# A decode attention kernel: the score products of a tile of keys in two halves, each on two column groups

## The chip, the cores and the metric

The kernel runs on one core of one Trainium2 chip. The core's engines work side by side, each through its own list of instructions in order, and wait for one another by semaphores. TensorE (PE) multiplies matrices into PSUM and loads its stationary operand with instructions of its own (PEld). VectorE (DVE) transposes and reduces, ScalarE (ACT) takes the exponential, SyncE (SP) issues the transfers from the chip's memory. The metric is the device time of one launch in microseconds (us), the median of the runs that are shown. An execution that the hardware profiler recorded gives the profile; its span runs from the first to the last instruction.

## The reference

One decode step for two batch rows: attention over the last 4,096 keys of a cache (32 query heads, 8 heads of keys and values) beside a gated feed-forward layer, both on the same normalised input, summed onto the input.

```python
xn = _layernorm(x)
q = (xn @ wq).reshape(B, Sq, Hq, Dh).transpose(0, 2, 1, 3)      # B=2, Sq=1, Hq=32, Dh=128
k = repeat(k_cache[:, :, Sk - W:, :], 4, axis=1)                # W=4096, 8 heads of keys
v = repeat(v_cache[:, :, Sk - W:, :], 4, axis=1)
p = softmax(einsum("bhqd,bhkd->bhqk", q, k) * Dh ** -0.5)
o = einsum("bhqk,bhkd->bhqd", p, v)
gate = xn @ W_gate; up = xn @ W_up
return x + o.reshape(B, Sq, Hq * Dh) @ wo + ((gate * (gate > 0)) * up) @ W_down
```

Everything is in 4-byte floats.

## The kernel before

All large inputs come through a ring of four buffers (`RING = 4`), each for one load of up to 4 MB, in the order in which they are used: wq in two loads, W_gate, W_up, then for each of four groups g two key tiles k and two value tiles v, then W_down and wo in two (the second in four pieces). SP issues a load when the buffer four loads earlier has been read for the last time: a key tile's buffer is free after its transposes, a value tile's after its products.

A group is one batch row with four of the eight heads of keys. Its score work runs over two key tiles, a = 0 and 1 (`scores`, L291). A key tile has 128 partitions of 64 positions by 128 numbers. DVE transposes it in 32 by 32 blocks, in two halves s1 = 0 and 1 (`S1` is 2) of two instructions each (L301), into a tile kT; kT has two buffers (`ktp`), so the halves of the next key tile write over those of this one, and must wait until PE has read them.

The products of q with a half are eight matmuls of 128 rows by 32 columns by 512 (L311): four blocks cb of the head dimension, which are summed, times two halves h of the positions. Each matmul appears twice in the trace, as PE takes two passes for it. The result lands in 32 of the 128 partitions of the scores tile ss[g], from `lo = 32 * (2 * s1 + h)` on. These four places are four column groups of the PE array: those of half 0 are groups 0 and 1, those of half 1 are groups 2 and 3. Matmuls on different column groups can run at the same time.

The order is that of the code (`manual_schedule`). Before, all four transposes of a key tile are issued, and then the sixteen matmuls with cb outermost, s1 next and h innermost, so that four in a row lie on the four column groups.

After the second key tile of a group follow the maximum over the scores (L319), a small chain through PE, DVE and ACT to the exponential (L340), a reordering product with a transpose (L346, L348), and for each value tile the products with p (`values`, L361). `gather` (L370, L376) masks and folds the result of a value tile, `finish` (L385, L386) scales it. The last gather and finish of a group are put into the list `late`, and run inside the next group's first call of `scores`, between the transposes of its first and second half. After group 1 the list also holds `spread_heads` (L391, L396), a set of small matmuls on PE and a copy on DVE.

At the end come the products with W_down and wo into y4 (L429), the last ones into y_ps (L436), a copy and the store.

Of the kernel before, what the change touches and what calls it, by code (L numbers as in the profile page):

```python
# [20 lines left out]
def kernel(  # L21
# [28 lines left out]
    S1 = W // (Q * 512)  # L50
    L = 32
    PB = P // L
    CB = DH // L
# [77 lines left out]
    qz = const.tile([P, NG, CB, 2, ZW], F32, name="qz")  # L131
# [98 lines left out]
    for r in range(R):  # L230
# [15 lines left out]
        for b in range(B):  # L246
            for pb in range(PB):
                rows = slice(L * pb, L * pb + L)
                for a in range(NP):
                    lo = 2 * a * 16 + pb * REP  # L250
# [35 lines left out]
    ss, pts, rls = {}, {}, {}  # L286
# [4 lines left out]
    def scores(g, a, kt_in):  # L291
        if a == 0:
            ss[g] = ps_s.tile([P, 512], F32, name=f"s{g}", tag="s")
        kts = []
        for s1 in range(S1):
            kt = ktp.tile([P, JH, CB, KL, 2], F32, name=f"kT{g}_{a}_{s1}", tag="kT")
            kts.append(kt)
            for n in range(2):
                lo = JH // 2 * n
                j = JH * s1 + lo  # L300
                nc.vector.transpose(  # L301
                    kt[:, lo:lo + JH // 2].rearrange("p j c k h -> p (j c k h)"),
                    kt_in[:, j * DH:(j + JH // 2) * DH],
                )
            while late:
                late.pop(0)()
        for cb in range(CB):
            for s1 in range(S1):
                for h in range(2):
                    lo = 32 * (2 * s1 + h)  # L310
                    nc.tensor.matmul(  # L311
                        ss[g][lo:lo + 32, :], qz[:, g, cb, h, 16 * a:16 * a + 32], kts[s1][:, :, cb, :, h],
                        start=(a == 0 and cb == 0), stop=(a == NP - 1 and cb == CB - 1),
                    )

# [82 lines left out]
    for g in range(NG):  # L398
        kt_in = [load_kv(k_cache, "k", g, a) for a in range(NP)]
        v_in = [load_kv(v_cache, "v", g, a) for a in range(NP)]  # L400
        for a in range(NP):
            scores(g, a, kt_in[a])
        turn(g, *softmax(g, maxima(g)))
        for a in range(NP):
            values(g, a, v_in[a])
            if a + 1 < NP:
                gather(g, a)
        late.append(lambda g=g: (gather(g, NP - 1), finish(g)))
        if g % B == 1 and g + 1 < NG:
            late.append(lambda g=g: spread_heads(g // B))  # L410
# [78 lines left out]
```

## Time and profile before

| | us |
|---|---|
| median of 3 runs | 252.2 |
| lowest and highest | 248.37 and 253.96 |
| the profiled execution | 251.82 |
| its span | 250.0 |
| PE busy, DVE busy | 153.1, 103.0 |
| loads from memory | 94.90 MB, 380 GB/s over the span |
| granted TensorE clock, mean | 0.816 |

The profile names groups of instructions by their line in the kernel, their engine, and the tiles as out<-in. "Idle before" is the time for which the engine stood still just ahead of an instruction, with what ended it. The granted clock is the share of full speed at which the array ran; in this trace it is either 0.50 or 1.00 at any moment. A matmul's shown duration is longer than the distance to the next one on the same column group, because consecutive ones overlap in the array: distances between starts say how fast they pass.

### The profile page before, as it was taken

The page shows a single profiled execution, that of the slowest core. Times are in us where ns is not written, and L with a number is a line of the kernel's source. Part 1 is how long each engine was busy: PE and PEld are TensorE (multiplying, and loading weights), DVE is VectorE, ACT ScalarE, POOL GpSimd, SP SyncE. Part 2 cuts the span into 40 slices and gives each one's busy share as a digit, 9 for nine tenths or more (in the row PEclk, how much of TensorE's full clock was granted, in tenths as well). Part 3 has the DMA queues.
Part 4 walks back from the last instruction along what each step waited for, and adds up shares of the span by engine and source line. Part 5 has one row for each costly group of instructions (what it writes and reads, how often), then busy time and mean ns, then how long its engine had stood idle before and what let it go on. Part 6 is the DMA issues. An engine that isn't in the chain of part 4 may idle for free.

```text
span 250.0 us, 2211 instructions
## 1 busy us (share of the span) xinstructions
PE 153.1 (61%) x948; PEld 49.2 (20%) x948; DVE 103.0 (41%) x121; ACT 8.3 (3%) x27; POOL 8.1 (3%) x31
## 2 busy tenths in 40 slices
PE   0079749316557585544588658185883817588993
PEld 0062342101001230101122321011220101122343
DVE  1220123295671267395225572912188292221201
ACT  0020213000000100000100000001000000100000
POOL 8400000000000000000000000000000000000000
PEclk9999977755757999795958957868599786959999
DMA  7999999999999999999999999999169999946900
GB/s 289 452 435 393 436 440 422 456 446 425 417 415 419 440 456 435 427 419 419 419 440 430 438 440 425 419 398 425 47 252 453 456 399 450 419 176 241 404 28 1
DMA packets 3784, 95.03 MB, mean 380 GB/s; under 512 B 430, under 2 KB 448, under 8 KB 704
## 3 DMA queue, kind: packets, MB, share of 16 engines
q1 hardware_dynamic: 3756, 94.90, 89.3%
q8 instruction: 7, 0.11, 0.2%
q10 hardware_dynamic: 20, 0.01, 0.0%
q14 instruction: 1, 0.01, 0.0%
HBM read 94.90 MB, written 0.00 MB: 380 GB/s over the span
## 4 chain that ended last, share of the span: by engine, by line
PE 49%; DVE 28%; DMA 10%; issue 7%; POOL 3%; ACT 1%; POOLq 0%; ACTq 0%; DVEq 0%
DVE kT L301 19%; PE s L311 16%; PE o L361 14%; DMA k<-in_A_k_cache_dram 10%; PE pp L346 4%; PE y L429 4%; PE oa L376 3%; PE q_ps L224 3%; DVE on L370 2%; DVE pt L348 2%; PE op L391 2%; PE xt_ps L214 1%; ACT p L340 1%; DVE m L319 1%; PE y_ps L436 1%
## 5 line engine op out<-in xcount | busy, mean ns | idle before, releaser
L311 PE MATMUL s<-kT,qz 128*32 128x512 f32 x256 | 56.8, 865 | 49.6 <-DVE kT L301 49.6
L301 DVE STREAM_TRANSPOSE kT<-k 128x2048 f32<-128x2048 f32 x32 | 71.4, 2281 | 21.1 <-PE s L311 18.8
L361 PE MATMUL o<-v,pt 128*32 128x512 f32 x256 | 38.5, 708 | 4.8 <-DVE rl L352 4.8
L311 PEld LDWEIGHTS s<-kT,qz 128*32 128x32 f32 x256 | 11.0, 144 | 91.6 <-DVE kT L301 63.5
L370 DVE TENSOR_TENSOR on<-o,mask 128x512 f32<-128x512 f32 x8 | 5.5, 692 | 26.5 <-PE o L361 26.5
L361 PEld LDWEIGHTS o<-v,pt 128*32 128x32 f32 x256 | 10.6, 128 | 25.8 <-issue 20.6
L214 PE MATMUL xt_ps<-rep,xn 2*128 2x32 f32 x16 | 3.7, 400 | 13.8 <-DVE xn L208 13.8
L346 PE MATMUL pp<-p,perm 128*128 128x512 f32 x16 | 9.3, 707 | 4.7 <-ACT p L340 4.7
L376 PE MATMUL oa<-on,picks 128*16 128x512 f32 x16 | 8.3, 597 | 6.3 <-DVE on L370 6.3
L319 DVE TENSOR_REDUCE m<-s 128x1 f32<-128x512 f32 x4 | 2.8, 692 | 22.5 <-PE s L311 22.5
L348 DVE STREAM_TRANSPOSE pt<-pp 128x1024 f32<-128x1024 f32 x4 | 5.0, 1250 | 13.2 <-PE pp L346 13.2
L224 PE MATMUL q_ps<-wq,xnT 128*32 128x512 f32 x64 | 9.8, 782 | 0.5 <-DVE xnT L216 0.5
L340 ACT ACTIVATE p<-s,nm 128x512 f32<-128x512 f32 x4 | 2.7, 687 | 170.7 <-DVE nm L334 170.7
L214 PEld LDWEIGHTS xt_ps<-rep,xn 2*128 2x128 f32 x16 | 3.6, 320 | 13.8 <-issue 13.8
L251 DVE COPY qz<-rq 32x32 f32<-32x32 f32 x16 | 3.0, 187 | 7.1 <-ACT qz L251 7.1
L391 PE MATMUL op<-osb,spread 16*128 16x32 f32 x32 | 5.0, 314 | 1.1 <-DVE osb L386 1.1
L429 PE MATMUL y<-wo,oT 128*32 128x512 f32 x48 | 5.4, 594 | 0.0
L391 PEld LDWEIGHTS op<-osb,spread 16*128 16x128 f32 x32 | 4.8, 231 | 2.8 <-DVE osb L386 2.0
L239 DVE COPY qT<-qt 128x32 f32<-128x32 f32 x2 | 0.4, 192 | 11.8 <-PE qt L235 11.8
L261 PE MATMUL g_ps<-wg,xnT 128*32 128x448 f32 x32 | 4.8, 762 | 0.0
L385 DVE TENSOR_REDUCE su<-oa 16x128 f32<-16x512 f32 x4 | 2.7, 680 | 4.5 <-PE oa L376 4.5
L429 PE MATMUL y<-wd,hT 128*32 128x512 f32 x28 | 4.5, 595 | 0.0
(79 smaller groups left out, 62.7 us busy)
## 6 DMA issues: line engine op xcount, KB each, us to landing
k<-in_A_k_cache_dram SPq DMA_DIRECT2D x8, 4096.0 KB, 25.9
v<-in_A_v_cache_dram SPq DMA_DIRECT2D x8, 4096.0 KB
wq<-in_A_wq_dram SPq DMA_DIRECT2D x2, 4096.0 KB, 16.9
wo<-in_A_wo_dram SPq DMA_DIRECT2D x1, 4096.0 KB
wg<-in_B_W_gate_dram SPq DMA_DIRECT2D x1, 3584.0 KB
wu<-in_B_W_up_dram SPq DMA_DIRECT2D x1, 3584.0 KB
wd<-in_B_W_down_dram SPq DMA_DIRECT2D x1, 3584.0 KB, 19.3
wo<-in_A_wo_dram SPq DMA_DIRECT2D x1, 2048.0 KB
```

Of the source, the lines that this page charges most:

```text
L214: nc.tensor.matmul(xt_ps[:, o, kc, :], cols, rep.rearrange("r s b -> r (s b)"), start=True, stop=True)
L224: nc.tensor.matmul(q_ps[r][32 * c:32 * c + 32, :], xnT[:, 0, kc, :], wqt[kc // 2][:, kc % 2, n * 512:(n + 1) * 512], start=(kc == 0), stop ...
L301: nc.vector.transpose(kt[:, lo:lo + JH // 2].rearrange("p j c k h -> p (j c k h)"), kt_in[:, j * DH:(j + JH // 2) * DH],)
L311: nc.tensor.matmul(ss[g][lo:lo + 32, :], qz[:, g, cb, h, 16 * a:16 * a + 32], kts[s1][:, :, cb, :, h], start=(a == 0 and cb == 0), stop=(a ...
L319: nc.vector.tensor_reduce(out=m, in_=ss[g], op=ALU.max, axis=AX.X)
L346: nc.tensor.matmul(pp[:, h], perm[:, h], p, start=True, stop=True)
L348: nc.vector.transpose(pts[g].rearrange("p n j k -> p j n k"), pp.rearrange("p h y -> p y h"))
L361: nc.tensor.matmul(o[32 * q:32 * q + 32, :], pts[g][:, a * S1 + s1, j:j + 4, :].rearrange("p u k -> p (u k)"), v[:, lo:lo + 512], start=(s ...
L370: nc.vector.tensor_tensor(ons[a], os[a].rearrange("p (u d) -> p u d", u=4), mask[:, :, None].to_broadcast([P, 4, P]), op=ALU.mult)
L376: nc.tensor.matmul(oa[g], picks[:, a].rearrange("p h a i -> p (h a i)"), ons[a], start=(a == 0), stop=(a == NP - 1))
L391: nc.tensor.matmul(op, spread[:, e].rearrange("h k e -> h (k e)"), osb[r][:, :, e * NJ:(e + 1) * NJ].rearrange("h b j -> h j b"), start=(e ...
L429: nc.tensor.matmul(y4[32 * t:32 * t + 32, :], lhsT.rearrange("p b s -> p (b s)"), w, start=(i < Q), stop=(i >= EARLY - Q))
```

## The change

The products with a half of a key tile are issued right behind the transposes of that half, instead of behind the transposes of both. Where the order was cb, s1, h it is now s1, cb, h: eight matmuls on column groups 0 and 1, then eight on groups 2 and 3. The number of instructions, their shapes and their data stay; so do the lists of DVE and SP, apart from the line numbers.

```diff
     def scores(g, a, kt_in):
         if a == 0:
             ss[g] = ps_s.tile([P, 512], F32, name=f"s{g}", tag="s")
-        kts = []
         for s1 in range(S1):
             kt = ktp.tile([P, JH, CB, KL, 2], F32, name=f"kT{g}_{a}_{s1}", tag="kT")
-            kts.append(kt)
             for n in range(2):
...
             while late:
                 late.pop(0)()
-        for cb in range(CB):
-            for s1 in range(S1):
+            for cb in range(CB):
                 for h in range(2):
                     lo = 32 * (2 * s1 + h)
                     nc.tensor.matmul(
-                        ss[g][lo:lo + 32, :], qz[:, g, cb, h, 16 * a:16 * a + 32], kts[s1][:, :, cb, :, h],
+                        ss[g][lo:lo + 32, :], qz[:, g, cb, h, 16 * a:16 * a + 32], kt[:, :, cb, :, h],
                         start=(a == 0 and cb == 0), stop=(a == NP - 1 and cb == CB - 1),
                     )
```

On PE, the first key tile of group 0 stands in the program before as follows; kT0_0_0 is the first half of its transposed keys and kT0_0_1 the second, s0 the scores of the group, qz the query, and the waits are in brackets:

```order
L311 MATMUL s0_333<-kT0_0_0_334,qz_94 32x512 [waits DVE_49]
L311 MATMUL s0_333<-kT0_0_0_334,qz_94 32x512
L311 MATMUL s0_333<-kT0_0_1_337,qz_94 32x512 [waits DVE_49]
L311 MATMUL s0_333<-kT0_0_1_337,qz_94 32x512
L311 MATMUL s0_333<-kT0_0_0_334,qz_94 32x512 x2
L311 MATMUL s0_333<-kT0_0_1_337,qz_94 32x512 x2
L311 MATMUL s0_333<-kT0_0_0_334,qz_94 32x512 x2
L311 MATMUL s0_333<-kT0_0_1_337,qz_94 32x512 x2
L311 MATMUL s0_333<-kT0_0_0_334,qz_94 32x512 x2
L311 MATMUL s0_333<-kT0_0_1_337,qz_94 32x512 x2
```

Of the eight products with the first half, two stood ahead of the wait for the second half and six behind it. In the changed program the same place on PE, with the second key tile (kT0_1_0 and kT0_1_1) and the transpose of the maximum behind it, reads:

```order
L308 MATMUL s0_333<-kT0_0_0_334,qz_94 32x512 [waits DVE_49]
L308 MATMUL s0_333<-kT0_0_0_334,qz_94 32x512 x7
L308 MATMUL s0_333<-kT0_0_1_345,qz_94 32x512 [waits DVE_49]
L308 MATMUL s0_333<-kT0_0_1_345,qz_94 32x512 x7
L308 MATMUL s0_333<-kT0_1_0_356,qz_94 32x512 [waits DVE_49]
L308 MATMUL s0_333<-kT0_1_0_356,qz_94 32x512 x7
L308 MATMUL s0_333<-kT0_1_1_367,qz_94 32x512 [waits DVE_49]
L308 MATMUL s0_333<-kT0_1_1_367,qz_94 32x512 x7
L318 MATMUL mt0_380<-ident_89,m0_378 1x128 [waits DVE_49]
```

All eight products of a half now stand behind the wait for that half alone.

The second place is on PE where group 2 begins, behind the last fold of group 1 (oa1) and the matmuls of `spread_heads` (op0). Before:

```order
L376 MATMUL oa1_545<-on1_1_576,picks_125 16x512 [waits DVE_49]
L391 MATMUL op0_582<-osb0_456,spread_111 128x32 [waits DVE_49]
L391 MATMUL op0_582<-osb0_456,spread_111 128x32 x7
L311 MATMUL s2_572<-kT2_0_0_573,qz_94 32x512 x2
L311 MATMUL s2_572<-kT2_0_1_592,qz_94 32x512 [waits DVE_49]
L311 MATMUL s2_572<-kT2_0_1_592,qz_94 32x512
L311 MATMUL s2_572<-kT2_0_0_573,qz_94 32x512 x2
```

and in the changed program:

```order
L373 MATMUL oa1_545<-on1_1_576,picks_125 16x512 [waits DVE_49]
L388 MATMUL op0_582<-osb0_456,spread_111 128x32 [waits DVE_49]
L388 MATMUL op0_582<-osb0_456,spread_111 128x32 x7
L308 MATMUL s2_572<-kT2_0_0_573,qz_94 32x512 x8
L308 MATMUL s2_572<-kT2_0_1_600,qz_94 32x512 [waits DVE_49]
L308 MATMUL s2_572<-kT2_0_1_600,qz_94 32x512 x7
```

The first half's products still follow the small matmuls of `spread_heads`, now all eight of them and with no wait of their own.

## The prediction

> **What bounds the kernel now.** I read the chain of waits first, then the groups of instructions, then the timeline of two groups. From the page: the span, what the chain consists of by engine, and the costliest DVE group.
>
> ```profile
> span 250.0 us, 2211 instructions
> PE 49%; DVE 28%; DMA 10%; issue 7%; POOL 3%; ACT 1%; POOLq 0%; ACTq 0%; DVEq 0%
> L301 DVE STREAM_TRANSPOSE kT<-k 128x2048 f32<-128x2048 f32 x32 | 71.4, 2281 | 21.1 <-PE s L311 18.8
> ```
>
> PE and DVE take turns: together 77% of the chain, transfers 10%. The last row says that DVE stood still 18.8 us ahead of key transposes because PE had not yet read the buffer. The timeline of group 0's first key tile and of all of group 1 shows where (start, length, engine, operation, idle time before and its releaser).
>
> ```profile
> 50.55 8.89 DVE L301 STREAM_TRANSPOSE kT<-k 128x2048 f32<-128x2048 f32 x4 [2.36 <-DMA k<-in_A_k_cache_dram]
> 55.12 1.92 PE L311 MATMUL s<-kT,qz 128*32 128x512 f32 x4 [7.78 <-DVE kT L301]
> 59.50 6.17 PE L311 MATMUL s<-kT,qz 128*32 128x512 f32 x28 [2.47 <-DVE kT L301]
> 64.82 8.89 DVE L301 STREAM_TRANSPOSE kT<-k 128x2048 f32<-128x2048 f32 x4 [5.38 <-PE s L311]
> ...
> 97.99 4.49 DVE L301 STREAM_TRANSPOSE kT<-k 128x2048 f32<-128x2048 f32 x2
> 102.53 5.19 PE L311 MATMUL s<-kT,qz 128*32 128x512 f32 x28 [4.63 <-DVE kT L301]
> 106.88 8.89 DVE L301 STREAM_TRANSPOSE kT<-k 128x2048 f32<-128x2048 f32 x4 [4.40 <-PE s L311]
> 111.44 1.12 PE L311 MATMUL s<-kT,qz 128*32 128x512 f32 x4 [3.72 <-DVE kT L301]
> 115.82 5.37 PE L311 MATMUL s<-kT,qz 128*32 128x512 f32 x28 [3.27 <-DVE kT L301]
> 121.25 0.69 DVE L319 TENSOR_REDUCE m<-s 128x1 f32<-128x512 f32 x1 [5.48 <-PE s L311]
> ```
>
> Strict alternation: transposes, then 28 of the 32 matmuls, meanwhile DVE idle (5.38 us in group 0, 4.40 in group 1, by the total (18.8 - 5.38) / 3 = 4.5 in each later group), then transposes again while PE is idle.
>
> The transfers do not set this pace, but they are close. A window of the steady part (DMA share and GB/s last):
>
> ```profile
> 60.00:175.00 115.00, 72.27 (x367) 19.72 (x359) 56.15 (x49) 2.33 (x6) 0.00 (x0) 0.78 1.00 427
> ```
>
> The load of k2_0, with its time from issue to landing,
>
> ```profile
> L73 SPq DMA_DIRECT2D k<-in_A_k_cache_dram x1: 534/534/534, 102.5 to 102.5; - x1
> DMA to landing us min/median/max: 26.1/26.1/26.1
> ```
>
> and that of k3_1:
>
> ```profile
> L73 SPq DMA_DIRECT2D k<-in_A_k_cache_dram x1: 535/535/535, 163.5 to 163.5; - x1
> DMA to landing us min/median/max: 14.1/14.1/14.1
> ```
>
> The DMA engines are busy all of that window at 427 GB/s, so a 4 MB tile (4.19 MB) takes 9.8 us. k2_0 landed at 102.5 + 26.1 = 128.6, and four loads earlier k1_0 at about 89.4. k3_1 landed at 163.5 + 14.1 = 177.6, and k3_0 9.8 earlier at 167.8. The first transposes of groups 1 and 2 started at:
>
> ```profile
> 90.56 2.30 DVE L301 STREAM_TRANSPOSE kT<-k 128x2048 f32<-128x2048 f32 x1
> ...
> 134.80 4.49 DVE L301 STREAM_TRANSPOSE kT<-k 128x2048 f32<-128x2048 f32 x2
> ```
>
> k1_0 was used about 1 us after landing, k2_0 6.2 us after. The ring then ran full; the loads of v3_0 and of wo's second half were issued at:
>
> ```profile
> 182.03 0.54 SPq L73 DMA_DIRECT2D v<-in_A_v_cache_dram  x1
> ...
> 226.40 1.85 SPq L448 DMA_DIRECT2D wo<-in_A_wo_dram  x4
> ```
>
> v3_0 could go only 4.4 us after the last load had landed. Compute is late, and gets later with each group.
>
> **The change part by part.** *How fast a pair runs.* Only two column groups work in a stretch now. The second round of two pairs:
>
> ```profile
> 55.97 1.06 PE L311 MATMUL s<-kT,qz 128*32 128x512 f32 x2
> 111.90 0.66 PE L311 MATMUL s<-kT,qz 128*32 128x512 f32 x2
> ```
>
> Against the starts at 55.12 and 111.44, a round of two takes 0.85 us at clock 0.50 and 0.46 at 1.00. A round of four takes no more: the 28 matmuls from 59.50 are seven rounds of four in 6.17 us, 0.88 each. So half of PE's width is given up: a half is 8 matmuls, 16 passes, eight rounds of two, 7 x 0.46 + 0.66 = 3.9 us at full clock, and 7 x 0.85 + 1.06 = 7.0 at half. It has 4.49 us of transposes (row 97.99) to hide behind: hidden at full clock, not at half.
>
> *Group 1, the model group.* On PE its first products (s) stand behind the last fold of group 0 (oa):
>
> ```profile
> 96.00 0.60 PE L376 MATMUL oa<-on,picks 128*16 128x512 f32 x1 [0.83 <-DVE on L370]
> 96.02 0.62 PE L311 MATMUL s<-kT,qz 128*32 128x512 f32 x1
> 96.44 0.59 PE L376 MATMUL oa<-on,picks 128*16 128x512 f32 x1
> 96.47 1.42 PE L311 MATMUL s<-kT,qz 128*32 128x512 f32 x3
> ```
>
> They start at 96.0 and, behind 0.9 us of oa on the same column group, end near 100.8, while DVE transposes the second half until 102.5. The 4.40 us wait at 106.88 goes: buffer 0 is read by then, and the second key tile's transposes follow at once. What is late next is DVE itself: 8.89 us of transposes, under which PE hides its half. Behind the last transpose stood 5.37 us of PE (row 115.82); now 3.9. Gain 4.40 + 1.5 = 5.9 us.
>
> *Does the clock hold?* Windows cut where the granted clock changes (PE busy is the second number, the clock the third from the end):
>
> ```profile
> 95.23:98.64 3.41, 1.89 (x6) 0.37 (x6) 2.22 (x4) 0.00 (x0) 0.00 (x0) 1.00 1.01 432
> 98.64:102.06 3.42, 0.00 (x0) 0.00 (x0) 3.42 (x2) 0.00 (x0) 0.00 (x0) 1.00 0.92 388
> 102.06:105.47 3.41, 2.94 (x16) 0.77 (x20) 0.41 (x1) 0.00 (x0) 0.00 (x0) 0.50 0.98 423
> 105.47:108.88 3.41, 2.25 (x16) 0.34 (x8) 2.00 (x1) 0.00 (x0) 0.00 (x0) 1.00 1.07 461
> 139.60:143.02 3.42, 1.70 (x8) 0.78 (x9) 1.54 (x3) 0.00 (x0) 0.00 (x0) 1.00 1.08 460
> 143.02:146.43 3.41, 3.41 (x16) 2.42 (x15) 1.00 (x2) 0.00 (x0) 0.00 (x0) 0.50 1.05 452
> 146.43:149.84 3.41, 0.81 (x2) 0.00 (x0) 3.41 (x2) 0.00 (x0) 0.00 (x0) 0.50 0.98 423
> ```
>
> The clock of a window follows from the window before. A window with 1.89 us of PE work, mostly on one or two column groups, kept 1.00; an empty one lost it; one with 2.94 us on four groups brought it back; 1.70 us lost it. In groups 1 to 3 the pairs fill 3.9 of every 4.49 us, far above 1.89, so a clock that is at 1.00 stays there, and PE no longer idles through whole transposes. Whether pairs alone bring a lost clock back no row shows: the nearest, 143.02, was full (small matmuls of `spread_heads`, then pairs) and did not. In the Trainium skill, the page "TensorE: Matmul & The Clock Gate", Part 1, says that an idle window of about 3.4 us drops the clock to half and about 3.4 us of sustained activity restores it; row 98.64 agrees with the first, row 143.02 does not with the second. By that page alone group 2's penalty below would be bounded by one window.
>
> *Group 2* enters at clock 0.50 (row 143.02), which I expect again, since `spread_heads` stays ahead of it. If pairs do not wake the clock, almost its whole gain goes (first rival); if one window of them does, the first half ends about 1 to 2 us after the transposes that should cover it. I take 1.5, since the pairs are long streams like the fours of 102.06 that did wake it. Gain 4.5 + 1.5 - 1.5 = 4.5. *Group 3* like group 1: 6.0. *Group 0* starts cold; but whatever it gains, group 1 cannot start before k1_0 lands: at most about 1 us; I take 0.7.
>
> *Nothing else moves.* DVE's and SP's lists are the same, and the new waits of PE have behind them only products that need the same half.
>
> **The sum.** Group 2's start gains 0.7 + 5.9 = 6.6, but k2_0 lands at 128.6, so 134.80 can move to 128.7 only: 6.1. Then 6.1 + 4.5 = 10.6 at group 3 (k3_0, at 167.8, is there before it), and 10.6 + 6.0 = 16.6 at its end. The value products keep their length; the tail behind them moves as a whole, if its loads are there: v3_0's load could go at 182.03 - 10.6 = 171.4, before k3_1 has landed, so the gap closes. From 177.6 on, 20.4 MB (v3_0, v3_1 and wo's two loads at 4.19, W_down at 3.67) take 48 us at 427 GB/s: the last piece is there at 225.5, as its buffer is free by 226.40 - 16.6 = 209.8. The last products end just ahead of the final copy,
>
> ```profile
> 247.15 0.29 DVE yo L459
> ```
>
> which moves to 230.6, so the loads are in time. Span 250.0 - 16.6 = 233.4; with the 1.8 us that the execution (251.82) has around its span 235.2. The median (252.2) is 0.4 above the profiled execution: 235.6, rounded to **236**.
>
> **The rivals.** *Pairs hold the clock but never wake it.* Then group 2 runs at half clock: half 1 of tile 0 is ready 4.5 us into the group's second transposes and takes 7.0, the next transposes to this buffer wait for it, then transposes and products follow, 4.5 + 7.0 + 4.5 + 7.0 = 23.0 us against 23.3 before (97.99 to 121.25). Group 2's gain falls from 4.5 to 0.3: 240. For it speaks row 143.02. If the clock is lost in all groups, little more than this 0.3 per group is left, about 251; row 95.23 speaks against it.
>
> *Slower: the clock is lost and the halves run one behind the other.* PE then needs 32 rounds of 0.85 = 27.2 us per group: from 96.0 to 123.2 against 121.2 in group 1, and from 55.1 to 82.3 in group 0 against some 79.9 (64.82 + 8.89 + 6.17); 2 to 2.4 us in each, about 9 in four: 261. It decides once a round takes more than 4.49 / 8 = 0.56 us and the other two column groups cannot start meanwhile. Against the second condition speak the rows of 96.00 to 96.47: a score pass started before the second pass of oa: column groups that are free run ahead, so late halves would overlap. In the Trainium skill, the same page, Part 3, says that matmuls keep program order in start and end, with no reordering; these rows go against it. By that rule a half-clock kernel would end at this rival's time.
>
> *The transfers become the bound.* If group 2 pays nothing for its clock, the end is where the loads allow it: 225.5 plus the last products, the copy and the store, 250.0 - 247.15 = 2.9 and about 0.5: 229 span, 231. That the change does not do what it says can be left out: each half's products stand behind the wait for that half only.
>
> **How the numbers follow.** The forecast (236, with its own range 231 to 240) has 0.55, the second clock case (240) 0.17, the transfer bound (231) 0.07, all groups cold (251) 0.11, slower (261) 0.10. A measurement of this kernel tells 2% from no change, about 5 us: below 247 is faster. Faster 0.55 + 0.17 + 0.07 = 0.79, same 0.11, slower 0.10. The range goes from 230, a little under the transfer bound, to 248, which leaves out the last two cases.
>
> **What would show it.** Right: the DVE idle time ahead of L301 released by PE falls from 18.8 us to a few, the last PE stretch ahead of each maximum is 3.9 us, the clock is 1.00 through the scores of groups 1 and 3, DVE waits once for k2_0 near 128.6, and the gap in the transfers near 180 is gone. Wrong: score passes spaced 0.85 us in group 1, a clock of 0.50 after a window full of pairs, or DVE transposes longer than 2.3 us while PE reads the same tiles.

## The result, and the profile after

| us | before | changed |
|---|---|---|
| median (6 runs each) | 251.84 | 234.73 |
| lowest to highest | 248.37 to 253.96 | 230.80 to 236.62 |
| span of the profiled execution | 250.0 | 229.0 |
| granted TensorE clock, mean | 0.816 | 0.902 |

The ratio is 0.930, with a 95% interval of 0.917 to 0.943. 236 was forecast, within 230 to 248. The profiled execution is the fastest of the six runs (230.80). Three of these six runs, and the execution of 235.47 us that a second profile below shows, are over 1.5% above that one, count as slow and are left out of the ratios (the medians keep them), and no conclusion rests on them alone.

From the page of the changed kernel: the chain by engine, and the groups of key transposes and value products (busy time, mean ns of one | idle time before and its releaser).

```profile
span 229.0 us, 2211 instructions
DMA 36%; PE 30%; DVE 24%; issue 5%; POOL 3%; ACT 1%; POOLq 0%; ACTq 0%; DVEq 0%
L299 DVE STREAM_TRANSPOSE kT<-k 128x2048 f32<-128x2048 f32 x32 | 71.2, 2275 | 11.1 <-DMA k<-in_A_k_cache_dram 8.4
L358 PE MATMUL o<-v,pt 128*32 128x512 f32 x256 | 32.0, 595 | 4.8 <-DVE rl L349 4.8
```

DVE hardly stands idle for PE ahead of the key transposes any more: of 18.8 us, 11.1 less 8.4 = 2.7 are left, most of them in group 0, and the rest of the idle time now waits for transfers. The transfers' share of the chain went from 10% to 36%, PE's from 49% to 30%. The last row had been 38.5 us and 708 ns in the kernel before:

```profile
L361 PE MATMUL o<-v,pt 128*32 128x512 f32 x256 | 38.5, 708 | 4.8 <-DVE rl L352 4.8
```

The value products got faster although nothing in them was changed.

Group 1 in the timelines of DVE and PE:

```profile
89.66 4.50 DVE L299 STREAM_TRANSPOSE kT<-k 128x2048 f32<-128x2048 f32 x2 [2.51 <-DMA k<-in_A_k_cache_dram]
...
97.21 13.26 DVE L299 STREAM_TRANSPOSE kT<-k 128x2048 f32<-128x2048 f32 x6
114.36 0.69 DVE L316 TENSOR_REDUCE m<-s 128x1 f32<-128x512 f32 x1 [3.89 <-PE s L308]
```

```profile
95.27 5.70 PE L308 MATMUL s<-kT,qz 128*32 128x512 f32 x15
101.75 3.64 PE L308 MATMUL s<-kT,qz 128*32 128x512 f32 x16 [0.77 <-DVE kT L299]
106.14 3.65 PE L308 MATMUL s<-kT,qz 128*32 128x512 f32 x16 [0.74 <-DVE kT L299]
110.52 3.80 PE L308 MATMUL s<-kT,qz 128*32 128x512 f32 x16 [0.74 <-DVE kT L299]
...
120.95 3.64 PE L358 MATMUL o<-v,pt 128*32 128x512 f32 x32 [1.21 <-DVE rl L349]
```

Six transposes run without a gap, and PE works through each half under the transposes of the next, waiting 0.7 us for each. From the second half's transposes to the maximum it is 17.15 us (97.21 to 114.36) where it was 23.26 (97.99 to 121.25).

### The profile page after: what moved, and what is told of

Same layout as the page of the kernel before. It is cut to its first block, busy times and chain, and to the rows that moved or that the text cites. A ratio compares the mean times of both kernels' runs of the same rounds, so it can differ in the third digit from the quotient of the medians.

```text
span 229.0 us, 2211 instructions
## 1 busy us (share of the span) xinstructions
PE 157.7 (69%) x948; PEld 53.0 (23%) x948; DVE 102.7 (45%) x121; ACT 8.3 (4%) x27; POOL 8.1 (4%) x31
## 3 DMA queue, kind: packets, MB, share of 16 engines
q1 hardware_dynamic: 3756, 94.90, 96.8%
## 4 chain that ended last, share of the span: by engine, by line
DMA 36%; PE 30%; DVE 24%; issue 5%; POOL 3%; ACT 1%; POOLq 0%; ACTq 0%; DVEq 0%
DMA k<-in_A_k_cache_dram 36%; DVE kT L299 17%; PE o L358 6%; PE s L308 6%; PE y L426 4%; PE oa L373 3%; PE q_ps L224 3%; PE op L388 2%; PE pp L343 2%; DVE on L367 2%; PE xt_ps L214 2%; DVE pt L345 1%; PE y_ps L433 1%; DVE su L382 1%; ACT p L337 1%
## 5 line engine op out<-in xcount | busy, mean ns | idle before, releaser
L308 PE MATMUL s<-kT,qz 128*32 128x512 f32 x256 | 64.9, 656 | 18.7 <-DVE kT L299 18.7
L299 DVE STREAM_TRANSPOSE kT<-k 128x2048 f32<-128x2048 f32 x32 | 71.2, 2275 | 11.1 <-DMA k<-in_A_k_cache_dram 8.4
L358 PE MATMUL o<-v,pt 128*32 128x512 f32 x256 | 32.0, 595 | 4.8 <-DVE rl L349 4.8
L308 PEld LDWEIGHTS s<-kT,qz 128*32 128x32 f32 x256 | 14.8, 116 | 65.1 <-issue 36.5
L373 PE MATMUL oa<-on,picks 128*16 128x512 f32 x16 | 9.5, 680 | 11.7 <-DVE on L367 11.7
L358 PEld LDWEIGHTS o<-v,pt 128*32 128x32 f32 x256 | 9.5, 109 | 20.4 <-issue 15.2
L343 PE MATMUL pp<-p,perm 128*128 128x512 f32 x16 | 10.7, 805 | 4.7 <-ACT p L337 4.7
L388 PE MATMUL op<-osb,spread 16*128 16x32 f32 x32 | 5.6, 335 | 1.1 <-DVE osb L383 1.1
L388 PEld LDWEIGHTS op<-osb,spread 16*128 16x128 f32 x32 | 5.3, 256 | 3.7 <-DVE osb L383 2.8
L373 PEld LDWEIGHTS oa<-on,picks 128*16 128x16 f32 x16 | 0.9, 95 | 18.3 <-DVE on L367 18.3
L343 PEld LDWEIGHTS pp<-p,perm 128*128 128x128 f32 x16 | 3.2, 222 | 7.6 <-issue 3.9
```

What stands on the lines that cost most here:

```text
L299: nc.vector.transpose(kt[:, lo:lo + JH // 2].rearrange("p j c k h -> p (j c k h)"), kt_in[:, j * DH:(j + JH // 2) * DH],)
L308: nc.tensor.matmul(ss[g][lo:lo + 32, :], qz[:, g, cb, h, 16 * a:16 * a + 32], kt[:, :, cb, :, h], start=(a == 0 and cb == 0), stop=(a == N ...
L343: nc.tensor.matmul(pp[:, h], perm[:, h], p, start=True, stop=True)
L358: nc.tensor.matmul(o[32 * q:32 * q + 32, :], pts[g][:, a * S1 + s1, j:j + 4, :].rearrange("p u k -> p (u k)"), v[:, lo:lo + 512], start=(s ...
L373: nc.tensor.matmul(oa[g], picks[:, a].rearrange("p h a i -> p (h a i)"), ons[a], start=(a == 0), stop=(a == NP - 1))
L388: nc.tensor.matmul(op, spread[:, e].rearrange("h k e -> h (k e)"), osb[r][:, :, e * NJ:(e + 1) * NJ].rearrange("h b j -> h j b"), start=(e ...
```

## The experiments

The theory had three terms: the buffer is read early, so DVE does not wait (a); less PE work is left behind the last transpose (b); and, from comparing the two profiles, PE keeps its clock into the value products (c). The kernel before had a median of 252.31 us beside the first four kernels, and of 253.53 us beside the last four. The times of single terms below are differences of these medians.

### The new order in the first key tile alone

```diff
+        early = a == 0
         for s1 in range(S1):
...
+            if early:
+                for cb in range(CB):
+                    product(s1, cb)
-        for cb in range(CB):
-            for s1 in range(S1):
+        if not early:
+            for cb in range(CB):
+                for s1 in range(S1):
+                    product(s1, cb)
```

(`product` is the loop over h with its matmul.)

> The products by halves in the first key tile of each group alone; the second key tile keeps the old order, with all products behind all four transposes. My theory (the gain is the buffer that is read early, 4.4 to 4.5 us per group, plus 1.5 us per group of shorter products behind the last transpose): DVE no longer waits for PE ahead of the second tile's transposes, but the last stretch of products stays at 5.4 us, so 4 x 4.4 less what group 0 and group 2 lose to transfers and clock, 251.8 - 12 to 14 = 238 to 240 us. Rival, that the gain is mostly that PE never idles long enough to lose its clock: the second tile's four transposes still leave PE idle for several us, so little is gained, 246 to 250 us.

240.72 us, ratio 0.954 [0.948, 0.960], a little above the 238 to 240 of the theory and far from the rival's 246 to 250. The timeline of DVE in group 1:

```profile
97.68 4.49 DVE L311 STREAM_TRANSPOSE kT<-k 128x2048 f32<-128x2048 f32 x2
102.33 8.89 DVE L311 STREAM_TRANSPOSE kT<-k 128x2048 f32<-128x2048 f32 x4 [0.16 <-PE s L300]
116.61 0.69 DVE L328 TENSOR_REDUCE m<-s 128x1 f32<-128x512 f32 x1 [5.40 <-PE s L300]
```

The wait for the buffer is 0.16 us instead of 4.40, and the stretch behind the last transpose is still 5.4. The value products stayed as they were:

```profile
L370 PE MATMUL o<-v,pt 128*32 128x512 f32 x256 | 38.5, 706 | 4.8 <-DVE rl L361 4.8
```

This is term (a) by itself, 11.6 us, with no help from the clock in the value products.

### The new order in the second key tile alone

The same edit with `early = a == NP - 1`.

> The products by halves in the second key tile alone. My theory: DVE still waits 4.4 us in each group, the last stretch falls from 5.4 to 3.9 us: 1.5 us per group, 245 to 247 us; with the first experiment's gain it should add up to the change's 17 to 21 us. Rival (clock): PE works through the second tile's transposes and enters the maximum and the value products at full clock, which takes 2.2 us more off each group: 238 to 241 us.

243.84 us, ratio 0.966 [0.960, 0.971], between the two expectations. DVE in group 1, and the value products:

```profile
96.83 4.48 DVE L311 STREAM_TRANSPOSE kT<-k 128x2048 f32<-128x2048 f32 x2
106.79 8.89 DVE L311 STREAM_TRANSPOSE kT<-k 128x2048 f32<-128x2048 f32 x4 [5.47 <-PE s L300]
119.58 0.69 DVE L328 TENSOR_REDUCE m<-s 128x1 f32<-128x512 f32 x1 [3.90 <-PE s L300]
```

```profile
L370 PE MATMUL o<-v,pt 128*32 128x512 f32 x256 | 32.0, 595 | 4.8 <-DVE rl L361 4.8
```

The last stretch fell to 3.90 us as (b) says. The wait for the buffer stayed and grew to 5.47 us, since the first tile's products ran at half clock for longer here; that took most of (b) back in this group: 22.75 us from 96.83 to 119.58, against 23.26. The value products are all at full clock, 38.5 less 32.0 = 6.5 us. But the reordering product, which runs between the maximum and the value products, got slower; before and here:

```profile
L346 PE MATMUL pp<-p,perm 128*128 128x512 f32 x16 | 9.3, 707 | 4.7 <-ACT p L340 4.7
```

```profile
L355 PE MATMUL pp<-p,perm 128*128 128x512 f32 x16 | 12.6, 934 | 4.7 <-ACT p L349 4.7
```

That is 3.3 us back. Added up along the groups, the span of this profile is 7.8 us shorter than before (242.2 against 250.0). Of these, 4.8 lie behind the maxima of groups 1 to 3 and are (c), which the theory as first stated did not have. The other 3.0 are (b): group 1 starts 1.1 us earlier, and from first key transpose to maximum groups 1 and 3 take 0.6 and 1.7 us less, group 2 0.4 more. So (b) alone is worth about half of the 6 us expected, partly because DVE still waits for the buffer. The two experiments add up as expected: 11.6 and 8.5 are 20.1 us, and the changed kernel beside them gained 252.31 less 233.22 = 19.1.

### The clock alone

```diff
+    def fill(dst, n):
+        for _ in range(n):
+            nc.tensor.matmul(
+                dst, perm[:, 0], qz.rearrange("p g c h z -> p (g c h z)")[:, 0:512], start=True, stop=True
+            )
     def maxima(g):
...
+        pps[g] = ps_kt.tile([P, 2, 512], F32, name=f"pp{g}", tag="kt")
+        fill(pps[g][:, 0], 1)
...
+        fill(pps[g][:, 1], 1)
         nm = work.tile([P, 1], F32, name=f"nm{g}", tag="nm")
...
+        os[0] = ps_1.tile([P, 512], F32, name=f"o{g}_0", tag="o")
+        fill(os[0], 1)
         rls[g] = work.tile([HR, 1], F32, name=f"rl{g}", tag="rl")
```

> The kernel before with three added matmuls per group (a product of constants, overwritten before it is used) in the gaps of PE between the maximum and the value products, so that the clock need not drop there; nothing else moves. If the clock in this stretch is worth what the two profiles suggest (value products of the first tile 5.8 us before, 3.64 after), groups 1 to 3 gain up to 2.2 us each less about 0.3 for the added work: 245 to 248 us. If the clock there is no part of the gain (something else hides it): 251 to 253 us.

247.05 us, ratio 0.977 [0.971, 0.983]. Its groups of value products and key transposes:

```profile
L374 PE MATMUL o<-v,pt 128*32 128x512 f32 x256 | 32.0, 595 | 0.6 <-DVE rl L365 0.6
...
L301 DVE STREAM_TRANSPOSE kT<-k 128x2048 f32<-128x2048 f32 x32 | 71.4, 2281 | 22.4 <-PE s L311 20.0
```

Work that nobody uses makes the kernel before 5.3 us faster, with the buffer waits no shorter (20.0 us). The interval of the ratio ends well below 1, but it does not settle whether the gain is over 2%. Term (c) is real and separate from (a).

### The changed kernel again, and with the same fillers

> The changed kernel once more, for a second profile of it. Its runs so far go from 230.8 to 236.6 us and the profiled one was the fastest. If the spread is the clock (which windows of PE drop to half), a profile near 236 us shows value products or score passes at half clock in some group where the first profile had full clock; if it is the transfers, the passes are the same and the waits on DMA are longer.

233.22 us, ratio 0.921 [0.912, 0.929]. The profile fell on an execution of 235.47 us with a span of 233.7, 4.7 more than the first. Its value products in group 1, and all of them:

```profile
121.78 5.74 PE L358 MATMUL o<-v,pt 128*32 128x512 f32 x32 [1.20 <-DVE rl L349]
```

```profile
L358 PE MATMUL o<-v,pt 128*32 128x512 f32 x256 | 37.8, 693 | 4.8 <-DVE rl L349 4.8
```

They take 5.8 us more than in the first profile. With the fillers (the three added matmuls) of the last experiment in the changed kernel:

> The changed kernel with the three added matmuls per group between the maximum and the value products. Of its two profiles the faster had value products at full clock in all groups, the slower at 5.2 to 5.8 us in groups 1 to 3, and was 4.7 us longer. If that is the clock's phase, the fillers fix it: value products of 3.64 us in every group, runs that all lie near the fast end, 230 to 232.5 us, less spread than the 231 to 236 of the changed kernel. If the spread is something else, 232 to 236 us as before.

230.58 us (four runs, 230.28 to 231.63), beside 253.53 for the kernel before, ratio 0.911 [0.905, 0.916]. The value products are at 32.0 us, 595 ns, and the runs lie within 1.4 us where the first six of the changed kernel lie within 5.8. That points to this clock as a source of the changed kernel's spread, but does not show it: these runs were on another chip than the four of the changed kernel that gave 233.22 us, and the intervals of the two ratios overlap.

### Quarters, half the products, and where it ends

In the next kernel the last half of each group is cut again: the products follow each of its two transposes (`last` is the second half of the second tile, `products` the loops over cb and h on a range of the positions).

```diff
+                if last:
+                    products(kt, s1, lo, lo + JH // 2)
...
+            if not last:
+                products(kt, s1, 0, JH)
```

> The changed kernel, where the products of the last half of each group are cut again and issued behind each of its two transposes (256 of the 512 positions each, twice as many matmuls of half the length). The last stretch behind the last transpose should fall from 3.8 to about 2.0 us, 1.8 us per group. If compute still sets the end, 4 x 1.8 less what the waits for k1_0 and k2_0 take back, 229 to 232 us from a run of the slower kind; if the transfers set it (last load at about 225, 2.9 us behind the last copy), nothing goes below 230 us, and a run of the faster kind stays at 230 to 231.

230.30 us (230.19 to 230.67), ratio 0.909 [0.903, 0.915]. The last stretch fell as expected; the maximum of group 1, and all value products:

```profile
112.94 0.69 DVE L323 TENSOR_REDUCE m<-s 128x1 f32<-128x512 f32 x1 [2.04 <-PE s L298]
```

```profile
L365 PE MATMUL o<-v,pt 128*32 128x512 f32 x256 | 34.8, 644 | 4.8 <-DVE rl L356 4.8
```

Both expected ranges hold 230.3, so the time alone does not decide between them. The runs are even closer together than with the fillers, although the value products of this profile are in part slow. So value products at full clock are not the only way to a small spread; the earlier end of the scores may do it as well.

The next leaves out blocks 2 and 3 of the head dimension in the scores:

```diff
-            for cb in range(CB):
+            for cb in range(CB // 2):
                 for h in range(2):
```

> Leaves out half of the score products (blocks 2 and 3 of the head dimension), so it does not compute the reference; transposes, loads and all else stay. PE per half falls from 3.8 to 2.0 us, which no half then needs to hide. If the transfers are the bound now: 230 to 232 us. If the pairs (half of PE's width) are still what costs: 4 x 1.8 us less than the changed kernel, 226 to 229 us.

232.36 us (230.03 to 233.15), ratio 0.916 [0.905, 0.926]. Half of the score work gone, and not faster than the fillers or the quarters, which do all of it. The 226 to 229 of the case that the pairs still cost did not come, and the median is just above the 230 to 232 of the other. Its mean clock is 0.808, and its value products are slow again:

```profile
L358 PE MATMUL o<-v,pt 128*32 128x512 f32 x256 | 36.9, 679 | 4.8 <-DVE rl L349 4.8
```

Fillers and quarters together:

> Both edits together, fillers and quarters. By the transfer bound 230 to 231.5 us, hardly better than each alone, with the DMA engines busy up to the last load near 225 us; if compute is still the bound, about 1.8 us per group below the filled kernel, 226 to 229 us.

230.13 us (230.07 to 230.23), ratio 0.908 [0.903, 0.913], the best of the kernels run, by 0.5 us at most from the fillers or the quarters alone. The chain of waits of its last stretch (start, length, what):

```profile
202.41 17.45 DMA wo<-in_A_wo_dram
219.86 0.14 issue
219.99 1.96 PE y L446 x16
221.95 0.02 issue
221.98 0.70 DVE ys L472
222.68 0.04 issue
222.72 2.18 PE y_ps L453 x64
```

The chain follows the load of wo for 17 us, and behind it compute for the last 5. The queue of loads was busy for nearly all of the span:

```profile
q1 hardware_dynamic: 3756, 94.90, 97.2%
```

In the changed kernel's first profile this share is 96.8%, in the kernel before 89.3%. The transfers are the bound here: the expectation for compute as the bound, 226 to 229 us, did not come. This is the only one of the profiles in which PE waits for wo. With the fillers or the quarters alone, as in the changed kernel's first profile, the chain from the load of k2_0 to the end is compute, and their spans, 228.9 to 229.1 us, are within 1 us of this one's 228.3: they stop just short of the bound.

## Why the prediction was right, step by step

*The pair at full clock.* Predicted 3.9 us for eight rounds; 3.64 to 3.80 (rows 101.75 to 110.52).

*Group 1's gain* 5.9; measured 23.26 - 17.15 = 6.1. The first experiment shows the buffer wait inside it alone.

*Group 0 and the transfer caps.* Group 1 was to start at most about 1 us earlier, 0.7 taken: 90.56 became 89.66, after 2.51 us of waiting for k1_0. Group 2 was to start at 128.7, when k2_0 has landed. DVE's timeline there and at the maximum of group 2, changed kernel:

```profile
128.72 4.51 DVE L299 STREAM_TRANSPOSE kT<-k 128x2048 f32<-128x2048 f32 x2 [3.37 <-DMA k<-in_A_k_cache_dram]
...
140.59 4.49 DVE L299 STREAM_TRANSPOSE kT<-k 128x2048 f32<-128x2048 f32 x2
145.53 8.89 DVE L299 STREAM_TRANSPOSE kT<-k 128x2048 f32<-128x2048 f32 x4 [0.45 <-PE s L308]
158.31 0.69 DVE L316 TENSOR_REDUCE m<-s 128x1 f32<-128x512 f32 x1 [3.90 <-PE s L308]
```

and the kernel before:

```profile
145.53 4.50 DVE L301 STREAM_TRANSPOSE kT<-k 128x2048 f32<-128x2048 f32 x2
...
169.02 0.69 DVE L319 TENSOR_REDUCE m<-s 128x1 f32<-128x512 f32 x1 [5.58 <-PE s L311]
```

*Group 2's gain* was put at 4.5 with 1.5 us lost to a cold start. It gained 23.49 - 17.72 = 5.8; it did start cold, but DVE waited only 0.45 us for the late half.

*Does the clock hold, and do pairs wake it?* Windows of the changed kernel, group 1 and group 2 (PE busy second, clock third from the end):

```profile
91.86:95.27 3.41, 0.47 (x3) 0.18 (x5) 2.88 (x3) 0.00 (x0) 0.00 (x0) 1.00 1.05 452
95.27:98.69 3.42, 3.42 (x12) 0.80 (x9) 2.36 (x3) 0.00 (x0) 0.00 (x0) 0.50 0.98 422
98.69:102.10 3.41, 2.64 (x12) 0.57 (x10) 3.41 (x3) 0.00 (x0) 0.00 (x0) 1.00 0.99 418
...
139.65:143.06 3.41, 3.41 (x12) 1.32 (x14) 2.58 (x3) 0.00 (x0) 0.00 (x0) 0.50 1.03 442
143.06:146.47 3.41, 3.41 (x20) 0.77 (x18) 2.96 (x2) 0.00 (x0) 0.00 (x0) 1.00 1.05 452
```

Group 1 did not start warm, as was assumed: DVE's wait for k1_0 left PE idle, and the clock was lost. In the window of 95.27 the score passes of one column group were 0.85 us apart, which the prediction had named as a sign of being wrong; the half was still read 0.77 us before PE could start on the next, so nothing was lost by it. One window full of pairs brought the clock back, in group 1 and in group 2. The first rival, pairs that never wake the clock (240), is out. It had rested on the full window of 143.02 before, whose first part was the short matmuls of `spread_heads`; why that one did not count stays open. The Trainium skill's page "TensorE: Matmul & The Clock Gate", Part 1, has about 3.4 us of sustained activity as enough, and these windows agree.

*The slower rival* needed the halves to run one behind the other when cold. Group 0 is the cold case. PE at the moment when the second half's keys became ready (59.5), in a window that ends at 61.5:

```profile
58.66 3.23 PE L308 MATMUL s<-kT,qz 128*32 128x512 f32 x14
```

Fourteen passes started between 58.66 and 61.5, where rounds of two, 0.85 us apart, would have started eight: the four column groups worked side by side as soon as both halves were there. With that and the woken clock, nothing of this rival happened.

*The transfer bound* was put at 231 and given little chance; the changed kernel's fastest run stands at 230.80, and the last three kernels that compute everything at 230.1 to 230.6.

*The term that was mis-sized* is "the value products keep their length". In the profiled execution they went from 38.5 to 32.0 us, which is most of why its span is 229.0 and not the forecast 233.4. From group 2's maximum to group 3's first transposes, where the first of its value products lie, it is 10.98 us (158.31 to 169.29) where it was 13.62 (169.02 to 182.64), 2.6 us less; behind group 3's maximum, at 193.76 and before at 213.40, the rest of the span is 1.4 us shorter. In group 1 the same saving went into the wait for k2_0. Group 2's scores gave 1.3 us more than forecast, but 1.1 went to its slower start, 11.87 us from 128.72 to 140.59 against 10.73 from 134.80. The sum had read the clock for the scores only. That the median still lay near the forecast is partly luck: as the second profile (span 233.7) and the fillers suggest, the clock is lost ahead of the value products in part of the runs.

## What to carry to other kernels

Where two engines hand a double buffer back and forth, let the reader take each buffer in the order in which it is filled, even if that halves the width at which it works: a slower product that is covered costs nothing, and the earlier release is the gain. It pays as long as the half-width work is shorter than what covers it, so read the clock in the window where it will run. And when compute has come within a few us of the loads, stop: the next edits measure the transfers.

## What the runs showed of the hardware that was not expected

The clock does not always outlive the stretch between the maximum and the value products, in which PE does little, and PE's busy time alone does not tell when. The kernel before, in the window of 3.41 us that holds this stretch in group 1, and in the next:

```profile
122.54:125.95 3.41, 1.78 (x6) 0.97 (x6) 0.48 (x4) 0.78 (x2) 0.00 (x0) 1.00 1.07 461
125.95:129.36 3.41, 2.21 (x12) 0.53 (x14) 1.29 (x2) 0.00 (x0) 0.00 (x0) 0.50 1.07 461
```

The changed kernel:

```profile
115.75:119.17 3.42, 1.89 (x6) 0.97 (x6) 0.42 (x3) 0.78 (x2) 0.00 (x0) 1.00 1.03 441
119.17:122.58 3.41, 2.20 (x20) 0.66 (x22) 1.29 (x2) 0.00 (x0) 0.00 (x0) 1.00 0.89 384
```

The same six passes, cut a little differently by the window: 1.78 us of work lost the clock, 1.89 kept it. It is no plain threshold of busy time, though. In group 0 of the kernel with the new order in the first key tile alone, the same six passes with 1.78 us kept it:

```profile
76.93:80.35 3.42, 1.78 (x6) 0.97 (x6) 0.46 (x4) 0.78 (x2) 0.00 (x0) 1.00 0.94 402
80.35:83.76 3.41, 2.20 (x20) 0.66 (x22) 1.29 (x2) 0.00 (x0) 0.00 (x0) 1.00 1.00 432
```

And 1.56 us of pairs in group 0 of the changed kernel were enough:

```profile
64.55:67.97 3.42, 1.56 (x8) 0.47 (x10) 3.42 (x2) 0.00 (x0) 0.00 (x0) 1.00 0.89 371
67.97:71.38 3.41, 2.71 (x14) 0.60 (x12) 2.77 (x2) 0.00 (x0) 0.00 (x0) 1.00 1.03 442
```

What decides stays open. But less PE work is not always the faster choice: the kernel with half of the score products had slow value products in three of its four groups, and three matmuls per group whose result is thrown away are worth 5.3 us in the kernel before.
